# Two-stage attention and a rational feed-forward block: the denominator as |h| times a factor made by GpSimd, and a word's sign mask made by ScalarE

## The chip, the core and the metric

The kernel runs on one core of a Trainium2 chip. The core has a TensorE (PE in the profile; PEld is its loading of weights, which overlaps the matmuls), a VectorE (DVE), a ScalarE (ACT), a GpSimd (POOL) and a SyncE (SP), which here only issues DMAs. The metric is the device time of one execution in microseconds. Matmuls write to PSUM, which DVE and ACT read and POOL does not use; everything else is in SBUF.

## The reference, cut to what matters

```python
def sm_attn(qq, kk, vv):                       # float32, 8 batches x 8 heads, head size 64
    s = scale * np.matmul(qq, kk.transpose(0, 1, 3, 2))
    s = s - np.max(s, axis=-1, keepdims=True)
    a = np.exp(s)
    a = a / (np.sum(a, axis=-1, keepdims=True) + 1e-09)
    return np.matmul(a, vv)
p_packed = sm_attn(p, k, v)                    # 32 packed queries, 576 keys
x = sm_attn(q, p_packed, p_packed)             # 576 queries, 32 packed keys -> 4608 x 512 tokens
h = x @ w_in                                   # 512 -> 2048, w_in is float64
P = a[0] + a[1] * h + a[2] * h2 + a[3] * h3    # h2 = h*h, h3 = h*h*h
Q = 1.0 + np.abs(b[0]) * np.abs(h) + np.abs(b[1]) * h2
out = (P / (Q + 1e-06)) @ w_out                # 2048 -> 512, w_out is float64
```

The two weight matrices arrive as 64-bit floating-point words and have to be turned into 32-bit ones on the chip. The factor 8 on several inputs makes the numbers large; the kernel carries the polynomials scaled by S = 2**-40.

## The kernel before, in words

**Units.** The feed-forward part is cut into 128 units: 8 batches (`bb`), 2 halves of 288 tokens (`x`), 8 chunks of 256 hidden features (`c`). `hidden(bb, x, c)` does one unit in steps. For each half `f` of 128 features, PE sums `h` (128x288) in one of two PSUM banks; ACT reads `h` three times and writes `Y` (a3 h + a2), `U` (b0 |h|) and `sq` (the square, scaled by the root of b1); DVE makes `Y = Y h`, then `Y = (Y + a1) h`. After the second half POOL adds `U = U + sq` over 128x576; ACT takes Ln of U plus a constant and Exp of minus that, which gives an approximate reciprocal `V` in PSUM; DVE adds a0 and multiplies by V, refines V by one Newton step with `V = (U + c) V` and `Y = (2 - V) Y`. ACT rounds Y to `gh`, POOL subtracts to get `gl`, and `acc_block`, three units later (`LAG`), multiplies both with the weights of `w_out`. The first 12 units (`PLAIN`) instead use full float32 matmuls and need no gh and gl. `U` has two buffers, `sq` one, `Y` three, `V` one, `h` two.

**The scales.** `constants()` prepares the numbers. The scale a3 of `Y`, b0 of `U` and the root of b1 of `sq` are loaded into ScalarE registers (`reg_a3`, `reg_b0`, `reg_root`); the root takes a small chain of one-column operations on the tile `root`. The bias a2 and the operands a0, a1 are [128, 1] pointers into `abS`.

**The words.** `convert()` turns 16 blocks of 128x1024 words into float32, 8 of `w_in` and 8 of `w_out`. With `hi` and `lo` the two 32-bit halves of a word: ACT rescales `hi` as a float, ACT scales `lo` as an unsigned integer into the destination, DVE masks the sign bit of `hi` into `lo` (TENSOR_SCALAR in the profile), DVE shifts `hi` by three and ors the sign in (SCALAR_TENSOR_TENSOR), and DVE adds the two integers (CUSTOM_DVE_ANT_0; ISA in the order). The raw words lie in tiles called `m` and `w`, which serve other purposes later; the results go to `win`, `w` or `half`.

**The attention** of batch bb+1 is spread over 16 steps (`attention`, `filler`) among the units of batch bb; for batch 0 it stands ahead of everything and is the start of the program. `m_chunk` makes the matrices `m` that combine attention and `w_in`; `remainder` does the 64 rows of each batch that don't fill a tile of 128; `divide` splits the float32 blocks of `w_out` into a rounded part and a rest (ACT, then POOL on `w` and `half`).

**The order.** A class `Planner` collects all instructions, prices each (`cost`), builds the dependences (`edges`) and simulates the engines as lists: `schedule` forward with a rank for each instruction, then backward from the ends, which gives new ranks. `order` repeats this `ROUNDS` times and keeps the order with the earliest modelled end; `SLACK` is added to each hop between engines in the backward pass; `shares` names instructions of DVE that are modelled as locking GpSimd out of SBUF. Each engine then executes its instructions strictly in that order. Where the model sees PE without work in the first 150 us, `idle` puts matmuls with the tile `zero` there, which change no sum. All instructions go through one helper, so the profile shows one line, L288, for nearly all, and they are told apart by the names of their tiles.

Of the kernel before, what the change touches and what calls it, by code (L numbers as in the profile page):

```python
# [31 lines left out]
class Planner:  # L32
# [26 lines left out]
    FIRST = {"tensor": 700.0, "vector": 800.0, "scalar": 2000.0, "gpsimd": 1400.0, "sync": 700.0}  # L59
    ROUNDS = 8  # L60
    SWITCH = 95
    SLACK = 150
    IN_FLIGHT = 8
# [30 lines left out]
    def cost(self, engine, name, args, kwargs):  # L94
# [7 lines left out]
        if engine == "scalar":  # L102
            fixed += (aps[-1].space == PSUM) * -42 + ("accum_out" in kwargs) * 93 + ("bias" in kwargs) * 93
            per += 0.1 * any(x.ap[-1][0] == 2 for x in aps[:2])
        if engine == "gpsimd" and len(aps) < 3:
            fixed, per = 135, 0.9
        if engine == "vector" and len(aps) > 2 and any(self.columns(x) == 1 for x in aps[1:]):
# [82 lines left out]

    def schedule(self, before, after, rank, back=False):

# [13 lines left out]
        while left:  # L206
            for e in self.ENGINES:
# [26 lines left out]
                for j in after[i]:  # L234
                    need[j] -= 1
                    f = self.ops[j][0]
                    way = self.WAY.get((f, e) if back else (e, f), self.PASS)
                    way += self.SLACK * (back and way > 0)
                    at[j] = max(at[j], end[i] + way)
# [9 lines left out]
    def order(self):  # L249
# [7 lines left out]
        for i, x in enumerate(before):  # L257
            for j in x:
                after[j].append(i)
        rank = list(range(n))  # L260
        best = None
        for r in range(self.ROUNDS):
            start, end = self.schedule(before, after, rank)
            if best is None or max(end) < best[0]:
                best = self.best = max(end), start, end
            s, e = self.schedule(after, before, [-x for x in end], True)
            m = max(e)
            rank = [m - x for x in e]
            rank[: self.pinned] = range(-self.pinned, 0)
        self.end, self.start = best[0], best[1]  # L270
# [49 lines left out]
def attention_rational_ffn(  # L320
# [46 lines left out]
    make_identity(tc.nc, ident)  # L367
    ab, abS, one, root = (sb.tile([P, n], F32, name=x) for n, x in ((6, "ab"), (7, "abS"), (1, "one"), (5, "root")))
    zero = sb.tile([P, D], F32R, name="zero")
# [28 lines left out]
    def constants():  # L398
# [9 lines left out]
        nc.vector.tensor_scalar(m, m, 2.0**-126, None, ALU.max)  # L408
        nc.vector.tensor_scalar(e.bitcast(I32), m.bitcast(I32), 23, None, ALU.logical_shift_right)
        nc.vector.tensor_scalar(e.bitcast(I32), e.bitcast(I32), 127, None, ALU.add)  # L410
        nc.vector.tensor_scalar(p.bitcast(I32), e.bitcast(I32), 1, 23, ALU.logical_shift_right, ALU.logical_shift_left)
        nc.vector.reciprocal(i, p)
        nc.vector.tensor_scalar(m, m, i, i, ALU.mult, ALU.mult)
        nc.scalar.activation(r, m, AF.Ln)
        nc.scalar.activation(r, r, AF.Exp, scale=0.5)
        nc.vector.reciprocal(i, r)
        nc.vector.scalar_tensor_tensor(r, m, i, r, ALU.mult, ALU.add)
        nc.vector.tensor_scalar(abS[:, 6:7], r, p, 0.5 * S**0.5, ALU.mult, ALU.mult)
# [3 lines left out]
    a0, a1, a2, b0 = (abS[:, i : i + 1] for i in (0, 1, 2, 4))  # L422

    reg_a3, reg_b0, reg_b1, reg_root = (tc.nc.scalar.alloc_register(x) for x in ("a3", "b0", "b1", "root"))

# [65 lines left out]
    def convert():  # L491
# [384 lines left out]
    def hidden(bb, x, c):  # L876
# [5 lines left out]
        for f in range(2):  # L882
# [220 lines left out]
```

## Time and profile before

| | |
|---|---|
| median of 3 runs | 781.16 us (780.78 to 782.17) |
| profiled execution | 780.48 us, span in the trace 778.7 us |
| PE busy | 743.9 us, 96% of the span |
| DVE busy | 690.6 us, 89% |
| ACT busy | 654.8 us, 84% |
| POOL busy | 451.8 us, 58% |
| DMA | 56.04 MB, mean 72 GB/s |

The profiled execution is 1.8 us longer than its span (what lies before the first and behind the last instruction) and 0.7 us under the median. A busy share says how much of the span an engine's instructions cover; neighbouring instructions overlap a little on ACT and DVE, and the matmuls' ends are modelled, so 100% is full and 96% of PE is an average over a start with gaps and a body without.

### The profile page before, as it was taken

What the parts mean: (1) busy time and instruction counts of PE and PEld (TensorE: products, weight loads), DVE (VectorE), ACT (ScalarE), POOL (GpSimd) and SP (SyncE); (2) the same over time, 40 slices, a digit from 0 to 9 for tenths busy, and PEclk for the clock granted to TensorE, in tenths of its full rate; (3) what the DMA queues carried; (4) which work ended last, traced back from release to release, by engine and by line L of the source; (5) the groups of instructions that cost most, each with busy time, mean ns of one, the idle gap of its engine ahead of it and who ended that gap; (6) DMA issues with size and microseconds to landing.
All of it is one profiled execution on the core that took longest, in us unless ns stands there. A gap on an engine that the chain in (4) does not pass through costs nothing.

```text
span 778.7 us, 15003 instructions
## 1 busy us (share of the span) xinstructions
PE 743.9 (96%) x5350; PEld 569.8 (73%) x5350; DVE 690.6 (89%) x1295; ACT 654.8 (84%) x1464; POOL 451.8 (58%) x448
## 2 busy tenths in 40 slices
PE   2769999999999999999999999999999999999997
PEld 2435554678788787778788787778778787778886
DVE  4899999987998879998998889998999789998872
ACT  5889978998887988998897898998898798898881
POOL 0012357756695556765596556855586556856663
PEclk9979999999999999999999999999999999999999
DMA  9984260023601155022701128021801023000001
GB/s 299 369 272 145 103 122 28 1 86 53 105 1 55 45 60 98 1 86 38 120 1 55 45 38 120 1 64 41 112 27 55 34 46 40 14 12 17 28 0 42
DMA packets 152028, 56.04 MB, mean 72 GB/s; under 512 B 122256, under 2 KB 141200, under 8 KB 151952
## 3 DMA queue, kind: packets, MB, share of 16 engines
q1 hardware_dynamic: 151952, 55.07, 30.3%
q8 instruction: 42, 0.69, 0.4%
q14 instruction: 34, 0.28, 0.1%
HBM read 45.62 MB, written 9.44 MB: 71 GB/s over the span
## 4 chain that ended last, share of the span: by engine, by line
PE 71%; DVE 12%; ACT 11%; DMA 2%; issue 2%; POOL 1%; SPq 0%; DVEq 0%; ACTq 0%; POOLq 0%
PE acc L288 37%; PE h L288 22%; PE at L288 12%; DVE Y L288 4%; DVE w L288 2%; ACT V L288 2%; ACT Y L288 2%; DVE small L288 2%; DVE kx L288 2%; DMA nat<-in_k_dram 2%; ACT U L288 2%; ACT sq L288 1%; ACT half L288 1%; ACT w L288 1%; DVE V L288 1%
## 5 line engine op out<-in xcount | busy, mean ns | idle before, releaser
L288 POOL TENSOR_TENSOR U<-U,sq 128x576 f32<-128x576 f32 x128 | 184.9, 1444 | 102.1 <-ACT U L288 47.5
L288 PE MATMUL acc<-w,gh 128*128 128x512 f32 x736 | 236.9, 406 | 0.3
L288 PE MATMUL h<-AH,m 128*128 128x288 f32 x1024 | 200.6, 318 | 4.7 <-DVE Y L288 4.0
L288 PEld LDWEIGHTS h<-AH,m 128*128 128x128 f32 x1024 | 160.0, 189 | 45.8 <-DVE Y L288 24.5
L288 POOL TENSOR_TENSOR gl<-Y,gh 128x512 fp32r<-128x512 f32 x116 | 150.4, 1296 | 46.1 <-ACT gh L288 15.2
L288 PEld LDWEIGHTS acc<-w,gh 128*128 128x128 f32 x736 | 133.5, 188 | 44.0 <-issue 9.0
L288 ACT ACTIVATE Y<-h,abS 128x288 f32<-128x288 f32 x256 | 128.5, 518 | 25.0 <-PE h L288 20.1
L288 PE MATMUL acc<-w,gl 128*128 128x512 f32 x384 | 148.1, 412 | 0.2 <-DVE w L288 0.2
L288 ACT ACTIVATE sq<-h 128x288 f32<-128x288 f32 x256 | 108.9, 428 | 34.9 <-PE h L288 26.7
L288 DVE TENSOR_TENSOR Y<-Y,h 128x288 f32<-128x288 f32 x256 | 109.0, 444 | 26.7 <-ACT sq L288 11.6
L288 DVE SCALAR_TENSOR_TENSOR Y<-Y,abS,V 128x576 f32<-128x576 f32 x128 | 102.9, 804 | 27.5 <-ACT V L288 26.7
L288 DVE SCALAR_TENSOR_TENSOR Y<-Y,abS,h 128x288 f32<-128x288 f32 x256 | 124.7, 505 | 2.2
L288 ACT ACTIVATE U<-h 128x288 f32<-128x288 f32 x256 | 102.5, 432 | 11.2 <-DVE V L288 7.4
L288 ACT ACTIVATE V<-U,one 128x576 f32<-128x576 f32 x128 | 99.4, 777 | 10.8 <-DVE Y L288 7.9
L288 PE MATMUL h<-AL,m 128*128 128x288 f32 x448 | 96.0, 295 | 0.0
L288 DVE SCALAR_TENSOR_TENSOR V<-U,V 128x576 f32<-128x576 f32 x128 | 95.8, 749 | 0.0
L288 DVE SCALAR_TENSOR_TENSOR Y<-V,Y 128x576 f32<-128x576 f32 x116 | 86.3, 744 | 1.4
L288 PEld LDWEIGHTS acc<-w,gl 128*128 128x128 f32 x384 | 71.3, 188 | 20.1 <-issue 6.4
L288 ACT ACTIVATE V<-V 128x576 f32<-128x576 f32 x128 | 85.5, 668 | 0.4
L288 PE MATMUL acc<-half,gh 128*128 128x512 f32 x240 | 78.7, 409 | 0.0
L288 ACT CAST gh<-Y 128x512 fp32r<-128x512 f32 x116 | 73.7, 635 | 2.0 <-DVE Y L288 1.3
L288 PEld LDWEIGHTS h<-AL,m 128*128 128x128 f32 x448 | 71.8, 188 | 0.6 <-issue 0.5
(135 smaller groups left out, 955.5 us busy)
## 6 DMA issues: line engine op xcount, KB each, us to landing
w<-in_moe_w_out_dram SPq DMA_DIRECT2D x16, 512.0 KB, 4.4
out_dram<-half SPq DMA_DIRECT2D x15, 512.0 KB, 3.1
nat<-in_k_dram SPq DMA_DIRECT2D x48, 144.0 KB, 3.8
nat<-in_q_dram SPq DMA_DIRECT2D x48, 144.0 KB, 4.3
nat<-in_v_dram SPq DMA_DIRECT2D x24, 256.0 KB, 3.3
m<-in_moe_w_in_dram SPq DMA_DIRECT2D x8, 512.0 KB, 5.7
w<-in_moe_w_in_dram SPq DMA_DIRECT2D x8, 512.0 KB, 9.6
nat<-in_k_dram SPq DMA_DIRECT2D x4, 512.0 KB, 8.5
```

The lines of the kernel that those rows point to most:

```text
L288: getattr(getattr(self.nc, engine), name)(*args, **kwargs)
```

## The change

The denominator |b0| |h| + |b1| h*h becomes |h| (b0 + b1 |h|). ACT no longer writes `sq`; `U` is now |h| without a scale; POOL makes the factor with one TENSOR_SCALAR (times b1, plus b0, both [128, 1] pointers) into the tile that was `sq`, and a multiplication takes the place of the addition. The root and the ScalarE registers go away, so the scale of `Y` is a pointer too.

In `convert`, the sign mask is made by ACT: a leaky rectification (Prelu) of `hi` as a float with scale 2**-40 and a slope of 2**90 for negative values, written into the integer `lo`; positive words come out as 0 and negative ones as the lowest integer, which is the sign bit. It has to read `hi` ahead of the rescaling in place and write `lo` behind the scaling of `lo`, so the three ACT instructions stand in a new sequence.

The planner is changed with it: `SLACK` becomes five values that are each tried for 6 rounds in place of one value for 8; the one-input price of GpSimd (135 + 0.9 per column) now holds for its TENSOR_SCALAR with pointers; and `shares` now names every DVE instruction with two wide SBUF operands.

```diff
-    ROUNDS = 8
+    ROUNDS = 6
-    SLACK = 150
+    SLACK = 60, 100, 150, 220, 300
-        if engine == "gpsimd" and len(aps) < 3:
-            fixed, per = 135, 0.9
+        if engine == "gpsimd" and sum(self.columns(x) > 1 for x in aps) < 3:
+            fixed, per = (135, 0.9)
...
-        return name in ("tensor_scalar", "tensor_copy") or (name == "tensor_add" and aps[0].dtype == I32)
+        wide = sum(self.columns(x) > 8 for x in aps[1:])
+        return wide > 1 or name in ("tensor_scalar", "tensor_copy")
...
-        for r in range(self.ROUNDS):
-            start, end = self.schedule(before, after, rank)
+        for slack in self.SLACK:
+            start, end = first
+            for r in range(self.ROUNDS):
+                s, e = self.schedule(after, before, [-x for x in end], slack)
...
-        m, e, p, r, i = (root[:, n : n + 1] for n in range(5))
-        nc.vector.scalar_tensor_tensor(m, ab[:, 5:6], -1.0, ab[:, 5:6], ALU.mult, ALU.max)
...
-        for i, reg in enumerate((reg_a3, reg_b0, reg_b1, reg_root)):
-            nc.scalar.reg_load(reg, abS[0:1, 3 + i : 4 + i].bitcast(I32))
...
+        nc.scalar.activation(di, lo.bitcast(U32), AF.Copy, scale=2.0**-29)
+
+        nc.scalar.activation(lo, hi.bitcast(F32), AF.Prelu, scale=2.0**-40, alpha=2.0**90)
         nc.scalar.activation(hi.bitcast(F32), hi.bitcast(F32), AF.Copy, scale=REBIAS)
-
-        nc.scalar.activation(di, lo.bitcast(U32), AF.Copy, scale=2.0**-29)
-        nc.vector.tensor_scalar(lo, hi, -0x80000000, None, ALU.bitwise_and)
         nc.vector.scalar_tensor_tensor(hi, hi, 3, lo, ALU.logical_shift_left, ALU.bitwise_or)
         nc.vector.tensor_add(dst.bitcast(I32), hi, di)
...
-            nc.scalar.activation(y, h, AF.Identity, scale=reg_a3, bias=a2)
-            nc.scalar.activation(u, h, AF.Abs, scale=reg_b0)
-            nc.scalar.activation(U2[:, f, :], h, AF.Square, scale=reg_root)
+            nc.scalar.activation(y, h, AF.Identity, scale=a3, bias=a2)
+            nc.scalar.activation(u, h, AF.Abs)
...
             if f == 1:
-                nc.gpsimd.tensor_add(U, U, U2)
+                nc.gpsimd.tensor_scalar(U2, U, b1, b0, ALU.mult, ALU.add)
+                nc.gpsimd.tensor_mul(U, U, U2)
```

The new order at three places; the numbers behind a name count tiles and differ by one between the two programs. First ACT around unit 70 in the body of the program, before:

```order
L288 ACTIVATE sq_70_914<-h_139_915 128x288
L288 ACTIVATE U_70_911<-h_139_915 128x288
L288 ACTIVATE Y_70_913<-h_139_915,abS 128x288
L288 ACTIVATE V_69_902<-U_69_901,one 128x2x288
L288 CAST gh_62_918<-Y_68_888 128x512
L288 ACTIVATE V_69_902<-V_69_902 128x2x288
L288 ACTIVATE U_70_911<-h_140_917 128x288
L288 ACTIVATE kx_6_865,small<-at_131_899,small 128x288
L288 ACTIVATE kx_6_865,small<-at_132_900,small 128x288
L288 ACTIVATE sq_70_914<-h_140_917 128x288
L288 ACTIVATE Y_70_913<-h_140_917,abS 128x288
```

The same place after, from the first read of the same `h` on:

```order
L293 ACTIVATE U_70_910<-h_139_914 128x288
L293 ACTIVATE V_69_901<-U_69_900,one 128x2x288
L293 ACTIVATE Y_70_912<-h_139_914,abS 128x288
L293 ACTIVATE V_69_901<-V_69_901 128x2x288
L293 ACTIVATE kx_6_864,small<-at_131_898,small 128x288
L293 ACTIVATE U_70_910<-h_140_916 128x288
L293 ACTIVATE Y_70_912<-h_140_916,abS 128x288
L293 ACTIVATE kx_6_864,small<-at_132_899,small 128x288
```

From each `h` two reads are left of three; `U` stands first, and the rounding to `gh` has moved behind both reads of `Y`.

POOL in the same unit, before:

```order
L288 TENSOR_TENSOR U_70_911<-U_70_911,sq_70_914 128x576
L288 COPY G<-Y_69_903 128x2x32
L288 TENSOR_TENSOR gl_63_929<-Y_69_903,gh_63_928 128x512
L288 TENSOR_TENSOR U_71_920<-U_71_920,sq_71_923 128x576
L288 COPY G<-Y_70_913 128x2x32
```

and after:

```order
L293 TENSOR_SCALAR sq_70_913<-U_70_910,abS 128x576
L293 TENSOR_TENSOR U_70_910<-U_70_910,sq_70_913 128x576
L293 TENSOR_TENSOR gl_62_918<-Y_68_887,gh_62_917 128x512
L293 COPY G<-Y_69_902 128x2x32
L293 TENSOR_SCALAR sq_71_922<-U_71_919,abS 128x576
```

One instruction more per unit, and `gl` of an older unit now stands behind the U of unit 70.

DVE at the first unit of the program, where the conversion of words is under way, before:

```order
L288 TENSOR_SCALAR w_5_119<-w_5_119 128x1024
L288 TENSOR_TENSOR Y_1_127<-Y_1_127,h_1_129 128x288
L288 TENSOR_TENSOR Y_1_127<-Y_1_127,h_2_132 128x288
L288 SCALAR_TENSOR_TENSOR Y_1_127<-Y_1_127,abS,h_1_129 128x288
L288 SCALAR_TENSOR_TENSOR w_5_119<-w_5_119 128x1024
L288 SCALAR_TENSOR_TENSOR Y_1_127<-Y_1_127,abS,h_2_132 128x288
L288 TENSOR_SCALAR w_7_121<-w_7_121 128x1024
L288 ISA w_10_161<-w_5_119,w_10_161 128x2048
```

and after:

```order
L293 SCALAR_TENSOR_TENSOR w_4_117<-w_4_117 128x1024
L293 TENSOR_TENSOR Y_1_126<-Y_1_126,h_1_128 128x288
L293 ISA win<-w_4_117,win 128x2048
L293 SCALAR_TENSOR_TENSOR Y_1_126<-Y_1_126,abS,h_1_128 128x288
L293 TENSOR_TENSOR Y_1_126<-Y_1_126,h_2_131 128x288
L293 SCALAR_TENSOR_TENSOR Y_1_126<-Y_1_126,abS,h_2_131 128x288
L293 SCALAR_TENSOR_TENSOR w_5_118<-w_5_118 128x1024
L293 ISA w_10_160<-w_5_118,w_10_160 128x2048
```

Each block has lost its mask (TENSOR_SCALAR), and one block more than before is still being converted when the first unit begins: `w_4` was done by then, now it stands among the first unit's instructions.

More of the change, by code (lines that the diff above doesn't have):

```diff
@@ L104, in cost @@
             per += 0.1 * any(x.ap[-1][0] == 2 for x in aps[:2])
-        if engine == "gpsimd" and len(aps) < 3:
-            fixed, per = 135, 0.9
+        if engine == "gpsimd" and sum(self.columns(x) > 1 for x in aps) < 3:
+            fixed, per = (135, 0.9)
+            if name == "tensor_scalar":
+                fixed, per = (135, 0.9)
         if engine == "vector" and len(aps) > 2 and any(self.columns(x) == 1 for x in aps[1:]):
@@ L189, in edges, with schedule @@
         return edges
-    def schedule(self, before, after, rank, back=False):
+    def schedule(self, before, after, rank, back=0):
         n = len(rank)
@@ L237, in schedule @@
                     way = self.WAY.get((f, e) if back else (e, f), self.PASS)
-                    way += self.SLACK * (back and way > 0)
+                    way += back * (way > 0)
                     at[j] = max(at[j], end[i] + way)
@@ L259, in order @@
                 after[j].append(i)
-        rank = list(range(n))
+        first = self.schedule(before, after, list(range(n)))
         best = None
-        for r in range(self.ROUNDS):
-            start, end = self.schedule(before, after, rank)
[L264 to L269, printed above, removed]
+        for slack in self.SLACK:
+            start, end = first
+            for r in range(self.ROUNDS):
+                s, e = self.schedule(after, before, [-x for x in end], slack)
+                m = max(e)
+                rank = [m - x for x in e]
+                rank[: self.pinned] = range(-self.pinned, 0)
+                start, end = self.schedule(before, after, rank)
+                if best is None or max(end) < best[0]:
+                    best = self.best = max(end), start, end
         self.end, self.start = best[0], best[1]
@@ L367, in attention_rational_ffn @@
     make_identity(tc.nc, ident)
-    ab, abS, one, root = (sb.tile([P, n], F32, name=x) for n, x in ((6, "ab"), (7, "abS"), (1, "one"), (5, "root")))
+    ab, abS, one = (sb.tile([P, n], F32, name=x) for n, x in ((6, "ab"), (6, "abS"), (1, "one")))
     zero = sb.tile([P, D], F32R, name="zero")
@@ L404, in constants @@
         nc.vector.memset(one, (1.0 + 1e-6) * S)
-        m, e, p, r, i = (root[:, n : n + 1] for n in range(5))
-        nc.vector.scalar_tensor_tensor(m, ab[:, 5:6], -1.0, ab[:, 5:6], ALU.mult, ALU.max)
[L408 to L418, printed above, removed]
-        for i, reg in enumerate((reg_a3, reg_b0, reg_b1, reg_root)):
-            nc.scalar.reg_load(reg, abS[0:1, 3 + i : 4 + i].bitcast(I32))
-    a0, a1, a2, b0 = (abS[:, i : i + 1] for i in (0, 1, 2, 4))
-    reg_a3, reg_b0, reg_b1, reg_root = (tc.nc.scalar.alloc_register(x) for x in ("a3", "b0", "b1", "root"))
+    a0, a1, a2, a3, b0, b1 = (abS[:, i : i + 1] for i in range(6))
     words = [(kind, 2 * c, 2) for kind in ("in", "out") for c in range(NCH)]
```

## The prediction

> **What bounds the kernel now.** I first cut the span into stretches (busy time of each engine in each stretch), because the page's averages mix a start, a stage that converts words and a long body.
>
> ```profile
> core 0: us, PE busy (x) PEld busy (x) DVE busy (x) ACT busy (x) POOL busy (x), PEclk, DMA share, GB/s
> 0.00:36.00 36.00, 17.25 (x233) 12.51 (x234) 22.74 (x48) 24.32 (x42) 1.70 (x7) 0.95 1.01 333
> 36.00:57.00 21.00, 13.59 (x83) 7.91 (x84) 20.13 (x36) 17.70 (x34) 2.77 (x3) 0.76 0.87 276
> 57.00:143.00 86.00, 85.17 (x542) 46.02 (x541) 85.50 (x160) 77.14 (x164) 45.08 (x35) 1.00 0.35 96
> 160.00:757.00 597.00, 593.34 (x4332) 477.39 (x4332) 538.23 (x1014) 514.25 (x1182) 384.19 (x389) 1.00 0.25 48
> ```
>
> From 36 to 143 us DVE is the bound: 20.13 of 21 and 85.50 of 86 us. PE looks full from 57 us on too, but its ends are modelled, so the waits decide which of the two leads:
>
> ```profile
> ACT Y L288 <- PE h L288: 7.1, 6, 1.9
> PEld acc L288 <- issue: 13.0, 46, 0.8
> PEld h L288 <- DVE Y L288: 2.9, 6, 0.9
> ```
>
> Those are from 57 to 143 us: ACT waits 7.1 us for `h`, PE's loads have holes, and DVE itself waits for nothing over 0.4 us. DVE sets the pace, the others follow. In the body, 160 to 757 us, PE leads with 593 of 597 us and DVE has 59 us free. What PE still waits for there, in the groups of weight loads and in the waits of DVE:
>
> ```profile
> L288 PEld LDWEIGHTS h<-AH,m 128*128 128x128 f32 x879 | 133.4, 188 | 30.9 <-DVE Y L288 18.8 <-DVE kx L288 1.7 <-issue 1.4
> ...
> DVE Y L288 <- ACT V L288: 25.1, 41, 2.4
> DVE Y L288 <- ACT sq L288: 11.0, 15, 1.0
> DVE Y L288 <- ACT U L288: 9.1, 18, 1.0
> DVE Y L288 <- ACT Y L288: 4.1, 5, 0.9
> ```
>
> The loads of `h` wait 18.8 us for DVE to have read an `h` bank, and DVE waits 11.0 + 9.1 + 4.1 us for ACT at that same place: the round is PE, ACT, DVE, PE, with two banks. So ACT's reads of `h` reach the end of the program through at most 18.8 us, though ACT is not the fullest engine.
>
> **The change part by part.** The instructions concerned, by group:
>
> ```profile
> L288 POOL TENSOR_TENSOR U<-U,sq 128x576 f32<-128x576 f32 x128 | 184.9, 1444 | 102.1 <-ACT U L288 47.5 <-ACT sq L288 34.4 <-DVE Y L288 8.8
> L288 ACT ACTIVATE sq<-h 128x288 f32<-128x288 f32 x256 | 108.9, 428 | 34.9 <-PE h L288 26.7 <-POOL U L288 6.9 <-POOL gl L288 0.8
> L288 DVE TENSOR_SCALAR w<-w 128x1024 int32<-128x1024 int32 x12 | 9.0, 753 | 0.0
> L288 DVE TENSOR_SCALAR m<-m 128x1024 int32<-128x1024 int32 x4 | 2.8, 697 | 8.0 <-ACT win L288 8.0
> L288 POOL COPY G<-Y 128x64 f32<-128x64 f32 x116 | 27.7, 239 | 74.1 <-DVE Y L288 65.6 <-ACT half L288 5.3 <-PE acc L288 2.4
> L288 POOL COPY pn<-pn x8: 284/295/992, 13.6 to 517.1; 128x128 f32<-128x128 f32 x8
> ```
>
> ACT's and DVE's neighbours overlap, so on a full engine an instruction costs its distance to the next start, which the timeline gives:
>
> ```profile
> 48.24 0.45 ACT L288 ACTIVATE sq<-h 128x288 f32<-128x288 f32 x1
> 48.53 0.46 ACT L288 ACTIVATE U<-h 128x288 f32<-128x288 f32 x1
> ...
> 70.22 1.35 ACT L288 ACTIVATE w<-w 128x1024 f32<-128x1024 f32 x1
> 71.25 0.62 ACT L288 ACTIVATE sq<-h 128x288 f32<-128x288 f32 x1
> ...
> 53.48 0.50 ACT L288 ACTIVATE Y<-h,abS 128x288 f32<-128x288 f32 x1 [0.78 <-PE h L288]
> 53.88 0.40 ACT L288 ACTIVATE U<-h 128x288 f32<-128x288 f32 x1
> ...
> 86.52 0.69 DVE L288 TENSOR_SCALAR w<-w 128x1024 int32<-128x1024 int32 x1
> 87.13 0.15 DVE L288 TENSOR_TENSOR small<-small 128x4 f32<-128x4 f32 x1
> ...
> 75.26 2.01 POOL L288 TENSOR_TENSOR U<-U,sq 128x576 f32<-128x576 f32 x1 [4.74 <-ACT sq L288]
> ...
> 76.28 1.56 DVE L288 TENSOR_SCALAR w<-w 128x1024 int32<-128x1024 int32 x1
> 77.76 0.50 DVE L288 SCALAR_TENSOR_TENSOR Y<-Y,abS,h 128x288 f32<-128x288 f32 x1
> ```
>
> So a `sq` is worth 0.29 us of ACT, a 1024-wide ACTIVATE 1.03, and a mask 0.61 us of DVE; `Y` with one [128, 1] pointer takes 0.11 more than `sq` with none.
>
> *The scale of Y as a second pointer.* No row has two. Bounds: nothing, and the 0.11 us of the first pointer twice. I take 0.11 us, 256 times.
>
> *Prelu.* Not in the trace. Bounds: the 1.03 us of the same width, and 1.4 us, the longest that such rows stand on ACT (1.35 above). I take 1.03: nothing in the rows tells one function from another.
>
> *POOL's TENSOR_SCALAR over 576 columns with two pointers.* Not in the trace. The nearest one-input rows are the copies, 239 ns for 64 columns and 295 (the median) for 128: 0.875 ns a column, so 0.69 us for 576 as the low end; the high end is the two-input 1.44 us. I take 0.69, since it reads one tile. The multiplication costs what the addition did.
>
> Stage one, 36 to 143 us. I count 11 of the 16 masks there (the other five come while DVE waits for ACT or DMA, as the 8.0 us of the `m` group show): 10 of 0.61 and the one that took 1.48 to the next start, 7.6 us less on a full DVE. ACT gains 11 Prelu x 1.03 = 11.3 us and 30 pointers x 0.11 = 3.3 us and loses 30 `sq` x 0.29 = 8.7 us (15 units), so 5.9 us more. It has 3.3 + 8.9 = 12.2 us free in the two stretches; 6.3 us stay. The stage can shrink by at most 6.3 us before ACT is full, by 7.6 before DVE is as full as now. With both tight I take 5 us; bounds 0 (below) and 7.6.
>
> Ahead of it, 0 to 36 us: five Prelu more on ACT. By the order, eight 1024-wide ACTIVATEs come ahead of the first copy of the transposed keys where there were six; the extra two fall into ACT's waits for DMA:
>
> ```profile
> ACT m L288 <- DMA m<-in_moe_w_in_dram: 6.3, 3, 3.9
> ```
>
> Counting to the first unit's `Y`, three more are placed; the third lies among copies that PE and DVE wait for. I add 1 us (0 to 3.1). The root's chain, twelve one-column instructions of DVE, two of ACT and the register loads, goes; it lay beside this work, and I count it as nothing, since each is 0.2 us or less and the DVE waits here anyway. The planner's idle matmuls (`zero`) go from 19 rows to 38 in the order. I cost them at nothing because they stand where PE has no data; if PE had data, the 38 instructions of 4 us that the trace shows now would become 8.
>
> The body holds 110 units (`sq` on ACT, then on POOL, from 160 to 757 us):
>
> ```profile
> 160.00:757.00 597.00, 91.48 (x219) 156.38 (x110) 1.00 0.25 48
> ```
>
> 219 `sq` go and 0.11 us per `Y` comes: ACT has about 0.36 us less per unit. What that is worth is bounded by 18.8 us, PE's waits for DVE's `Y`, and by nothing. Where `sq` stood ahead of `Y` in the order (as in unit 70) DVE's two steps start 0.29 us earlier, and DVE's 11.0 us for `sq` vanish, while its 9.1 us for `U` may stay. I take 8 us, somewhat under half. PE's own arithmetic is unchanged, so nothing beyond the waits can be had there. If ACT's `U` is done earlier, the next to be late is POOL: its chain is one TENSOR_SCALAR longer. POOL has 384 of 597 us, and 110 x 0.69 make it 460, 77%. Who waits for POOL's U today, in the waits of the whole span:
>
> ```profile
> ACT sq L288 <- POOL U L288: 6.9, 12, 0.9
> ACT V L288 <- POOL U L288: 1.8, 2, 1.2
> ```
>
> The first was for the one `sq` buffer, which only POOL will use. The second says that Ln nearly always finds U done. In the order `U` is read off `h` first and `sq` no longer follows, 0.3 to 0.4 us earlier, so Ln sees some 0.3 us more delay; behind it in ACT's queue stand the next unit's reads of `h`. I count nothing for it, and cost it as a rival.
>
> Sum, against the profiled execution of 780.48 us (span 778.7 and 1.8 around it): -5 + 1 - 8 = -12, 768.5 us. The median of the runs lies 0.7 above that execution, so 769.2 us.
>
> **A rule against the change.** The pair at 75.26 and 76.28 us shows POOL's U at 2.01 us and DVE's mask, begun inside it, at 1.56 us where others take 0.69. The Trainium skill, page "SBUF — State Buffer", section "Who interferes with whom", says that DVE in a two-port mode, or with two SBUF inputs, shares a port pair with GpSimd that is locked for a whole instruction, and the second one "fully blocks". By that rule POOL's new instruction, which reads SBUF, opens more collisions with the two DVE steps of a conversion that stay; the trace agrees with it in this pair, where the mask lost 0.87 us. By the rule carried through all conversions the sum would be that of rival (b); by the rows' own durations it is the -12 above.
>
> **The rivals.**
>
> (a) *PE's floor.* In the body the waits of PE have another cause: DVE's 25.1 us for `ACT V` stay, and the `h` bank is released no earlier. For it: DVE's `Y` is not behind `sq` in all units. Then -5 + 1 = -4, 777.2 us.
>
> (b) *The port.* In stage one 22 DVE steps of conversions (two each for 11 blocks) remain, on a full DVE. If each loses 0.35 us to POOL, about what separates two such rows today (below), 7.7 us are gone and with them the 7.6 us of the masks: 0 + 1 - 8 = -7, 774.2 us. Against it: POOL is busy for only 45 of 86 us there.
>
> ```profile
> 103.75 1.57 DVE L288 SCALAR_TENSOR_TENSOR w<-w 128x1024 int32<-128x1024 int32 x1
> 58.33 1.22 DVE L288 SCALAR_TENSOR_TENSOR w<-w 128x1024 int32<-128x1024 int32 x1
> ```
>
> (c) *POOL becomes the bound: slower.* If the TENSOR_SCALAR costs 1.44 us, POOL gets 384 + 110 x 1.44 = 542 of 597 us, 91%, and more in the attention steps of each batch, where it has these besides:
>
> ```profile
> L288 POOL TENSOR_TENSOR kx<-kx,small 128x576 f32<-128x576 f32 x28 | 32.5, 1163 | 18.8 <-DVE small L288 18.8
> L288 POOL TENSOR_TENSOR AL<-kx,AH 128x576 fp32r<-128x576 f32 x14 | 20.1, 1436 | 1.8 <-ACT AH L288 1.8
> L288 POOL TENSOR_TENSOR gl<-Y,gh 128x512 fp32r<-128x512 f32 x116 | 150.4, 1296 | 46.1 <-ACT gh L288 15.2 <-PE acc L288 11.2 <-issue 10.4
> ```
>
> Eight units then need 8 x (1.44 + 1.44 + 1.30 + 0.24) + 4 x 1.16 + 2 x 1.44 = 42.9 us of POOL in 8 x 597/110 = 43.4 us. In a strict order an engine that is 99% full makes others wait; 2 us for each of seven batches, and no gain in the body: 14 - 5 + 1 = +10, 791.2 us. It decides from about 1.2 us per TENSOR_SCALAR, where these stretches are 95% full.
>
> (d) *The change does not do what it says.* Prelu at 1.4 us and the second pointer at 0.22 fill ACT: 15.4 + 6.6 - 8.7 = 13.3 us more against 12.2 free. ACT then keeps stage one as long as it is, the start loses 1, and the pointers eat most of the `sq` in the body: no change, 781 us.
>
> (e) *The whole of it.* All 18.8 us of PE's waits go, and 5 in stage one: 780.48 + 0.7 - 18.8 - 5 + 1 = 758.4 us.
>
> **How the numbers follow.** The forecast has 0.50, (a) 0.18, (b) 0.08, (c) 0.12, (d) 0.06, (e) 0.06. The likeliest is 769.2 us, with 765 to 773 as its own range (3 us less or more of the body's 8, 1 of stage one's 5). The range for the whole is 758 to 782: it holds all cases but (c) and the edges of (e) and (d). Faster by over 0.2% (1.6 us, about what a measurement of this kernel can tell from no change): the forecast, (a), (b) and (e), 0.82, less 0.02 for (a) falling short, 0.80. Slower: (c) and a third of (d), 0.14. The rest, 0.06, is within 0.2%.
>
> **What would show it.** DVE from 36 us to where it stops being full should end near 138 us in place of 143, with 16 fewer TENSOR_SCALARs of 128x1024; ACT should be over 95% there. POOL's TENSOR_SCALAR should read 0.6 to 0.8 us. PEld's wait of `h` for `DVE Y` should fall from 18.8 to about 10 us, and no engine should wait over some 5 us for `POOL U`. I am wrong if that last wait grows to tens of us (c), if DVE's conversion steps lengthen from 1.22 to 1.6 us throughout (b), or if stage one ends no earlier with ACT full (d).

## The result, and the profile after

The changed kernel takes 799.57 us (median of 4 runs, 798.46 to 799.77), the kernel before 780.97 us on the same chip: a ratio of 1.0233, with a 95% interval of 1.0221 to 1.0246. It is slower by 18.6 us where 12 us less were forecast. The profiled execution is the one of 798.46 us (span 796.7). All medians and ratios leave out two executions of some 4000 us, one of two_factors and one of the kernel before beside two_or. The stretches of the changed kernel, with the columns of the first fence of the prediction:

```profile
0.00:36.00 36.00, 15.22 (x232) 10.63 (x232) 19.05 (x36) 26.43 (x41) 1.46 (x7) 1.00 1.02 321
36.00:57.00 21.00, 13.84 (x98) 7.54 (x99) 16.56 (x28) 19.70 (x36) 5.67 (x5) 0.80 0.93 313
57.00:143.00 86.00, 85.41 (x548) 49.38 (x547) 81.43 (x151) 81.44 (x145) 47.96 (x41) 0.99 0.35 92
160.00:757.00 597.00, 586.25 (x4256) 461.46 (x4249) 522.06 (x992) 455.07 (x939) 456.70 (x482) 1.00 0.26 48
```

In stage one DVE is no longer full (16.56 of 21 and 81.43 of 86 us, before 20.13 and 85.50), as the removal of the masks should make it. In the body every engine but POOL is less busy than before: DVE 522, ACT 455, PE 586 us. POOL went from 384 to 457. No engine is full, so something waits. The chain of work that ended last, before and then after, shares of the span by engine:

```profile
PE 71%; DVE 12%; ACT 11%; DMA 2%; issue 2%; POOL 1%; SPq 0%; DVEq 0%; ACTq 0%; POOLq 0%
```

```profile
PE 31%; ACT 24%; DVE 18%; POOL 16%; issue 5%; DMA 4%; SPq 1%; POOLq 0%; ACTq 0%; DVEq 0%
```

PE carried 71% of that chain and now carries 31%; POOL went from 1 to 16%. The waits and groups that answer to those of the prediction:

```profile
POOL sq L293 <- ACT U L293: 108.8, 81, 5.1
ACT V L293 <- DVE Y L293: 40.3, 32, 3.4
ACT V L293 <- POOL U L293: 34.0, 34, 2.5
```

```profile
L293 POOL TENSOR_SCALAR sq<-U,abS x128: 811/823/1436, 48.5 to 776.2; 128x576 f32<-128x576 f32 x128
L293 PEld LDWEIGHTS h<-AH,m 128*128 128x128 f32 x848 | 126.7, 188 | 32.4 <-DVE Y L293 21.9 <-issue 1.2 <-DVE small L293 0.8
L293 ACT ACTIVATE w<-w 128x1024 int32<-128x1024 f32 x12 | 14.4, 1200 | 0.0
L293 ACT ACTIVATE w<-w 128x1024 f32<-128x1024 f32 x12 | 14.4, 1202 | 0.0
```

ACT's Ln waits 34.0 us in 34 places for POOL's U, where it waited 1.8 us in 2. POOL itself waits 108.8 us for ACT's U. Two engines that wait for each other, both with idle time, suggest a round, and the timelines of ACT and POOL show one, without another wait in between (a unit late in the body):

```profile
653.98 0.75 ACT L293 ACTIVATE V<-U,one 128x576 f32<-128x576 f32 x1 [0.61 <-POOL U L293]
654.75 0.64 ACT L293 ACTIVATE V<-V 128x576 f32<-128x576 f32 x1
655.30 0.41 ACT L293 ACTIVATE U<-h 128x288 f32<-128x288 f32 x1
655.59 0.60 ACT L293 ACTIVATE Y<-h,abS 128x288 f32<-128x288 f32 x1
656.07 0.42 ACT L293 ACTIVATE U<-h 128x288 f32<-128x288 f32 x1
...
659.03 0.75 ACT L293 ACTIVATE V<-U,one 128x576 f32<-128x576 f32 x1 [1.10 <-POOL U L293]
```

```profile
656.66 0.82 POOL L293 TENSOR_SCALAR sq<-U,abS 128x576 f32<-128x576 f32 x1 [1.29 <-ACT U L293]
657.57 1.43 POOL L293 TENSOR_TENSOR U<-U,sq 128x576 f32<-128x576 f32 x1
```

Ln at 653.98, Exp, U and Y of the next unit's first half, U of its second half until 656.49; POOL's factor from 656.66 and product until 659.00; the next Ln at 659.03. That is 5.05 us a unit, set by ACT and POOL in turn. It is not the pace of every unit: of the 109 distances from one Ln to the next in the body, 14 lie between 5.03 and 5.10 us and 20 are shorter.

To see where the 18.6 us are, I read the start of the first `Y` of three units from ACT's timeline (unit 18 is where the body begins; one profiled execution each):

| run | unit 0 | unit 18 | unit 127 | body, 18 to 127 | median |
|---|---|---|---|---|---|
| before | 47.6 | 161.6 | 757.3 | 595.7 | 780.97 |
| after | 46.7 | 164.0 | 775.9 | 611.8 | 799.57 |
| no_pointer | 46.2 | 162.1 | 766.7 | 604.6 | 790.43 |
| no_factor | 47.8 | 164.3 | 764.8 | 600.5 | 787.2 |
| no_pointer_no_factor | 46.9 | 162.1 | 757.7 | 595.6 | 780.37 |
| new_order | 51.4 | 163.7 | 762.9 | 599.1 | 783.05 |
| den_only | 50.7 | 168.5 | 783.5 | 615.0 | 804.62 |
| mask_relu | 53.2 | 162.0 | 760.0 | 597.9 | 778.58 |
| before_halves_Y4 | 49.5 | 163.8 | 759.6 | 595.8 | 783.21 |
| two_or | 46.4 | 161.6 | 755.7 | 594.1 | 779.15 |

The changed kernel loses 2.4 us up to unit 18 and 16.1 us in the body. The other rows are the experiments.

### The profile page after: what moved, and what is told of

Its sections match the earlier page's. It is cut to its first block, busy times and chain, and to the rows that moved or that the text cites. A ratio compares the mean times of both kernels' runs of the same rounds, so it can differ in the third digit from the quotient of the medians.

```text
span 796.7 us, 15046 instructions
## 1 busy us (share of the span) xinstructions
PE 752.4 (94%) x5388; PEld 568.5 (71%) x5388; DVE 677.0 (85%) x1269; ACT 615.5 (77%) x1222; POOL 552.4 (69%) x576
## 4 chain that ended last, share of the span: by engine, by line
PE 31%; ACT 24%; DVE 18%; POOL 16%; issue 5%; DMA 4%; SPq 1%; POOLq 0%; ACTq 0%; DVEq 0%
PE acc L293 15%; DVE Y L293 11%; PE h L293 10%; ACT V L293 9%; PE at L293 6%; POOL U L293 6%; ACT Y L293 4%; POOL sq L293 4%; ACT U L293 4%; DVE V L293 3%; POOL gl L293 3%; ACT w L293 2%; DMA m<-in_moe_w_in_dram 2%; ACT gh L293 2%; DVE kx L293 1%
## 5 line engine op out<-in xcount | busy, mean ns | idle before, releaser
L293 POOL TENSOR_SCALAR sq<-U,abS 128x576 f32<-128x576 f32 x128 | 106.1, 829 | 130.0 <-ACT U L293 108.8
L293 PEld LDWEIGHTS h<-AH,m 128*128 128x128 f32 x1024 | 157.9, 189 | 47.6 <-DVE Y L293 28.0
L293 POOL TENSOR_TENSOR U<-U,sq 128x576 f32<-128x576 f32 x128 | 183.8, 1436 | 9.5
L293 ACT ACTIVATE Y<-h,abS 128x288 f32<-128x288 f32 x256 | 148.8, 595 | 22.4 <-PE h L293 14.6
L293 ACT ACTIVATE V<-U,one 128x576 f32<-128x576 f32 x128 | 96.1, 751 | 81.1 <-DVE Y L293 40.3
L293 DVE TENSOR_TENSOR Y<-Y,h 128x288 f32<-128x288 f32 x256 | 112.6, 447 | 19.5 <-ACT U L293 11.2
L293 ACT ACTIVATE U<-h 128x288 f32<-128x288 f32 x256 | 100.9, 409 | 15.5 <-DVE V L293 9.1
L293 ACT CAST gh<-Y 128x512 fp32r<-128x512 f32 x116 | 72.0, 621 | 27.6 <-DVE Y L293 14.9
L293 ACT ACTIVATE V<-V 128x576 f32<-128x576 f32 x128 | 82.7, 646 | 0.8
```

Of the source, the lines that this page charges most:

```text
L293: getattr(getattr(self.nc, engine), name)(*args, **kwargs)
```

## The experiments

**Is it POOL's step or the order?** Two runs keep the order of all engines' instructions word for word and change only what POOL issues; two exchange the planner.

`no_factor`, at the place where an instruction is issued:

```diff
+                if engine == "gpsimd" and str(args[0].tensor.tag)[:2] == "sq":
+                    continue
+                # ... and the multiplication takes U, U in place of U, sq
```

> The changed kernel with every engine's order kept, but GpSimd's TENSOR_SCALAR is not issued and the multiplication takes U twice (the factor b0 + b1 |h| is left out, U becomes |h| squared). Chain theory (a unit's path U, POOL, Ln, Exp, Y got 0.83 us longer and the body pays for it): Ln's wait for POOL U falls from 34 us to under 5, the time falls by 12 to 18 us of the 18.6 lost, 782 to 788 us. Order theory (the sequence of the instructions is what costs): the time stays at 795 to 800 us though POOL has 106 us less to do.

`two_factors` issues that TENSOR_SCALAR twice.

> The changed kernel with every engine's order kept, and the TENSOR_SCALAR issued twice, so that POOL's chain per unit is another 0.83 us longer (POOL about 552 + 106 = 658 of the span). Chain theory: the loss of the 0.83 us is repeated or more, 815 to 830 us, and ACT's wait for POOL U grows from 34 to 60 us and more. Order theory: under 5 us more, 800 to 805 us, since POOL is not full.

`old_order` and `new_order` exchange `Planner` between the two kernels (the old one with the new one-input price of GpSimd).

> The changed arithmetic, ordered by the planner's old search (one slack of 150, 8 rounds) and old list of DVE instructions that lock GpSimd; GpSimd's one-input price as in the changed kernel. Order theory: 768 to 783 us, the loss is gone. Chain theory: 795 to 802 us, the loss stays whoever orders it.

> The arithmetic of before (ACT's square, POOL's addition, DVE's mask, registers), ordered by the changed planner (five slacks of 6 rounds, the longer list of locking DVE instructions). Order theory: 793 to 800 us, the loss comes with the search alone. Chain theory: 776 to 784 us, no loss without the longer POOL step.

Measured: no_factor 787.2 us (ratio 1.0067, 1.0046 to 1.0089), two_factors 881.42 (1.1276, 1.1249 to 1.1303), old_order 799.07 (1.0213, 1.0189 to 1.0238), new_order 783.05 (1.0029, 1.0014 to 1.0045). The order theory falls: the old search keeps the loss, and the new search without the new arithmetic costs 2 us. POOL's step matters, and not in proportion: taking one away gives 12.4 us, adding one costs 82, far over the 815 to 830 us that the chain theory expected. In two_factors the distance from Ln to Ln grows by the added step:

```profile
ACT V L294 <- POOL U L294: 133.6, 80, 3.5
...
729.01 0.75 ACT L294 ACTIVATE V<-U,one 128x576 f32<-128x576 f32 x1 [2.48 <-POOL U L294]
...
735.00 0.75 ACT L294 ACTIVATE V<-U,one 128x576 f32<-128x576 f32 x1 [2.21 <-POOL U L294]
```

5.99 us in place of 5.05, about the 0.83 of the step and the 0.09 of the gap behind it. The body of before needs 595.7 / 109 = 5.47 us a unit on average, so a round of 5.05 can hold back only units with little other work, and one of 5.99 nearly all. The distances from Ln to Ln bear that out in part. Over the last 16 units, which have no attention of a next batch beside them, they sum to 75.5 us before, 85.4 after and 99.3 in two_factors; from unit 18 to 111 to 515.1, 525.7 and 587.3. So 9.9 of the 20.5 us that the changed kernel loses by these starts lie in those 16 units. One reservation on no_factor: its multiplication of U by itself ran faster than that of two tiles (the row below, 1153 ns against 1436), so it took about 1.1 us off each unit's POOL work, not 0.83, and the factor alone is probably worth less than 12.4 us.

```profile
L297 POOL TENSOR_TENSOR U<-U 128x576 f32<-128x576 f32 x128 | 147.6, 1153 | 158.8 <-ACT U L297 156.2 <-DVE Y L297 1.6 <-POOL AL L297 0.8
```

**Which half of the change?** `den_only` puts DVE's mask back; `mask_relu` is the kernel before with the changed planner and the mask by ACT.

```diff
 den_only:
+        nc.scalar.activation(hi.bitcast(F32), hi.bitcast(F32), AF.Copy, scale=REBIAS)
         nc.scalar.activation(di, lo.bitcast(U32), AF.Copy, scale=2.0**-29)
-        nc.scalar.activation(lo, hi.bitcast(F32), AF.Prelu, scale=2.0**-40, alpha=2.0**90)
-        nc.scalar.activation(hi.bitcast(F32), hi.bitcast(F32), AF.Copy, scale=REBIAS)
+        nc.vector.tensor_scalar(lo, hi, -0x80000000, None, ALU.bitwise_and)
 mask_relu (on before): the reverse, with
+        nc.scalar.activation(lo, hi.bitcast(F32), AF.Relu, scale=2.0**-40)
```

> The changed denominator, scales and planner, with DVE's mask of before. If the denominator carries the whole loss: 797 to 803 us, and Prelu alone is worth the small rest either way. If the mask has a part in it (it should have gained 5 us by the forecast, or lost some 6 us that the run without the factor leaves unexplained): 804 to 808 us, or 792 to 795 us.

> The denominator, scales and registers of before, the changed planner, and the word's mask by ACT, with a plain rectification (Relu) in the place of Prelu, which leaves out the sign of negative words. The forecast's step for the mask (5 us less in stage one, 1 us more ahead of it): 4 us under the run that has the new order alone, 777 to 780 us. Rival: ACT's three steps of a conversion stand in one queue and DVE waits for the third, so nothing is won, 782 to 786 us.

den_only took 804.62 us (1.0303, 1.0274 to 1.0332), mask_relu 778.58 (0.9963, 0.9947 to 0.9979). So the mask by ACT gains 5.0 us (804.62 to 799.57) with the one denominator and 4.5 us (783.05 to 778.58) with the other, and the denominator carries more than the whole loss. All four are planned anew, so these differences hold what the order does too.

**Can the round be cut?** `u_first` adds one rule to the planner; `halves` shortens POOL's path.

```diff
 u_first:
+        for u, i in self.ln.items():                 # index of a unit's Ln
+            if u + 1 in self.read:                   # index of a unit's last read of h on ACT
+                edges[i].add(self.read[u + 1])
 halves:
-            if f == 1:
-                nc.gpsimd.tensor_scalar(U2, U, b1, b0, ALU.mult, ALU.add)
-                nc.gpsimd.tensor_mul(U, U, U2)
+            nc.gpsimd.tensor_scalar(U2[:, f, :], u, b1, b0, ALU.mult, ALU.add)
+            nc.gpsimd.tensor_mul(u, u, U2[:, f, :])
```

> The changed kernel, with one more rule for the planner: a unit's Ln stands on ACT behind the next unit's second read of h into U (in the changed kernel that read stands behind Ln in 98 of 109 units of the body). Loop theory (Ln, Exp, the next U, POOL's TENSOR_SCALAR and multiplication, Ln form a closed round of 5.05 us, which is longer than PE's work of a unit): the round is cut, ACT's wait for POOL U falls from 34 to under 8 us and the time to 780 to 788 us. Theory of the strict queues (wherever the reads stand, POOL's 0.83 us more per unit come out as another wait, as with the old search, where ACT waited 55 us for POOL gl): 794 to 800 us, with ACT or PE waiting for POOL gl instead.

> The changed kernel, but GpSimd does factor and multiplication for each half of 288 columns as soon as ACT has written it, four instructions of about 0.52 and 0.77 us in place of two of 0.83 and 1.44. From the second read of h to Ln there are then about 1.3 us of POOL in place of 2.27, though POOL has about 0.3 us more per unit (some 595 us busy of the span). Chain theory: 778 to 787 us. Theory of POOL's load (it is the work and not the length of the path that counts): 802 to 812 us.

u_first took 799.0 us (1.0231, 1.02 to 1.0262), halves 810.5 (1.0377, 1.0354 to 1.0401). The loop theory fails: ACT's wait for POOL U fell from 34.0 to 2.3 and 8.3 us, and nothing was gained. halves, which gave POOL 66 us more work, lies where the theory of POOL's load had it. Another wait has taken the place of the first, as the theory of the strict queues said (6.7 us in the changed kernel); u_first first, then halves:

```profile
ACT Y L297 <- POOL gl L297: 39.3, 37, 2.1
```

```profile
ACT Y L293 <- POOL gl L293: 72.5, 62, 2.6
```

(In old_order the same wait has 55.5 us.) `gl` is the last reader of a unit's `Y`, and `Y` has three buffers: ACT may not write `Y` before POOL has come to the `gl` of three units ago. So I asked whether it is POOL's work or the number of buffers. `extra_after_gl` adds work of nearly the same size off the path from U to Ln; `halves_Y4` is halves with a factor tile of 288 columns, which leaves room for a fourth `Y`.

```diff
 extra_after_gl, behind each issued gl:
+                    self.nc.gpsimd.tensor_scalar(self.again, self.again, 1.0, 0.0, ALU.mult, ALU.add)   # the last sq
 halves_Y4:
-    ... (("U", 2), ("sq", 1), ("Y", 3)))
+    ... (("U", 2), ("sq", 1), ("Y", 4)))
+    U2_ring = Ring(sb, "sq", 1, [P, HALF])
```

> The changed kernel with every engine's order kept, and one more TENSOR_SCALAR of 128x576 on GpSimd (times 1, plus 0, in place) behind each of its 116 subtractions gl: about the work that the doubled factor added (0.74 to 0.83 us a unit), but outside the path from a unit's U to its Ln. Theory of the path (a round of ACT and POOL in which POOL itself idles 1.28 us a unit): the extra falls into that idle time, 799 to 806 us. Theory of the load (POOL's work as such costs): 860 to 885 us, as with the factor doubled (883).

> The run with POOL's work in halves (810.5 us), and a fourth buffer for Y, made room for by a factor tile of 288 columns. There ACT waited 72 us for POOL gl, which reads Y before Y's buffer comes free. If it is the three buffers of Y that keep ACT in step with POOL: that wait falls under 20 us and the time to 785 to 797 us. If POOL's work is what counts, the wait moves elsewhere: 806 to 813 us.

```profile
L297 POOL TENSOR_SCALAR sq<-sq 128x576 f32<-128x576 f32 x116 | 78.8, 680 | 0.0
```

extra_after_gl took 821.88 us (1.0523, 1.0505 to 1.054): 22 us for 78.8 us of added work, where the same kind of work on the path cost 82 us for 106. Both theories missed: the place counts, but off the path is not free. POOL takes its instructions in order, so the added one also holds up the next unit's factor: Ln's wait for POOL U grew from 34.0 to 53.4 us. halves_Y4 took 790.2 us (1.0122, 1.0105 to 1.0138), 20 us under halves with the same POOL work (622.8 us busy, 79% of its span; 618.6 in halves), and `Y` now waits for PE instead of `gl`:

```profile
L293 ACT ACTIVATE Y<-h,abS 128x288 f32<-128x288 f32 x256 | 152.3, 599 | 56.9 <-PE h L293 49.7 <-POOL sq L293 1.2 <-POOL gl L293 1.1
```

That POOL is too full is thereby refuted. What costs, as far as these runs show, is the time from a unit's first instruction to the release of its buffers, over a fixed number of buffers; that no single hold explains the whole loss is what u_first showed.

`before_factor` adds the TENSOR_SCALAR to the kernel before, in its order, on `sq` ahead of the addition. `mask_ptr` is before with the changed planner, Prelu for the mask, and pointers for the three scales.

> The kernel before with every engine's order kept, and a TENSOR_SCALAR of 128x576 with two pointers on sq ahead of POOL's addition (which changes the denominator's value): the longer POOL step alone, with ACT's square, registers and DVE's mask as they were. If the POOL step carries the loss: 797 to 815 us. If the square's removal or the pointers on ACT have a part in it: under 792 us.

> The mask by Prelu with the old denominator (ACT's square, POOL's addition) and the changed planner; the three scales are [128, 1] pointers in place of registers, some 0.08 us more for each of 768 reads of h on ACT. If the mask's gain stands (the run with Relu had 778.6) and ACT has room for the pointers: 777 to 783 us. If ACT, then some 92% busy in the body, becomes the limit: 788 to 800 us.

before_factor took 822.92 us (1.0533, 1.0516 to 1.0551), above both expectations and above the changed kernel. Its order was planned without the step, and with `sq` on ACT a second wait comes up, for the one `sq` buffer; which of the two makes it slower than the changed kernel was not tested:

```profile
ACT sq L290 <- POOL U L290: 42.7, 45, 1.9
```

mask_ptr took 811.46 us (1.0389, 1.0372 to 1.0406), above both expectations and 33 us above mask_relu. It differs from that run in the pointers, in Prelu for Relu (1237 against 1253 ns on the blocks in `w`, so not dearer) and in the order planned with them:

```profile
L293 ACT ACTIVATE Y<-h,abS 128x288 f32<-128x288 f32 x256 | 157.5, 628 | 15.2 <-PE h L293 11.6 <-POOL gl L293 3.1
L293 ACT ACTIVATE sq<-h,abS 128x288 f32<-128x288 f32 x256 | 136.9, 538 | 20.6 <-PE h L293 14.1 <-POOL U L293 4.8 <-POOL G L293 1.2
L293 ACT ACTIVATE U<-h,abS 128x288 f32<-128x288 f32 x256 | 129.3, 535 | 5.0 <-DVE V L293 3.0 <-PE h L293 1.6
```

Each pointer adds about 0.11 us to a read of `h` (`sq` 428 ns before, 538 here). So Y's second pointer had to be a suspect in the changed kernel too.

**Pointer and factor at one order.** `no_pointer` keeps the order of the changed kernel and issues `Y` with the constant `S` for its scale; `no_pointer_no_factor` does that and no_factor together; `den_reg` is den_only with a3 in ACT's register.

> The changed kernel with every engine's order kept, and the scale of Y a constant in the instruction in place of a [128, 1] pointer (a3 is left out). Y's reads of h should fall from 595 to some 515 ns. If the pointer has a part in the loss (two Y reads lie between Exp and the second read of U in the round of 5.05 us, 0.16 to 0.22 us a unit): 785 to 794 us. If ACT's idle time, 23%, covers it: 797 to 801 us.

> The same with the TENSOR_SCALAR left out as well, every order kept (b0, b1 and a3 are left out). The run without the factor alone stood at 787.2, 6.6 us above before. If the pointer is the rest: 776 to 782 us. If the rest lies in the order or in the start: 785 to 788 us.

> The changed denominator with DVE's mask (804.6 us), and the scale of Y in a register of ACT as before; planned anew. If the pointer has a part: 792 to 799 us, and what stays above the run with the new order alone (783) is POOL's step. If not: 803 to 806 us.

```profile
L295 ACT ACTIVATE Y<-h,abS 128x288 f32<-128x288 f32 x256 | 125.3, 502 | 25.4 <-PE h L295 16.3 <-POOL gl L295 7.1 <-POOL U L295 1.3
```

```profile
L293 ACT ACTIVATE Y<-h,abS 128x288 f32<-128x288 f32 x256 | 148.8, 595 | 22.4 <-PE h L293 14.6 <-POOL gl L293 6.7 <-POOL G L293 0.2
```

The first row is no_pointer, the second the changed kernel: 502 against 595 ns. no_pointer took 790.43 us (1.012, 1.0093 to 1.0147), no_pointer_no_factor 780.37 (0.9989, 0.9975 to 1.0003), den_reg 798.55 (1.0214, 1.0188 to 1.0241). At one order the pointer costs 9.1 us, POOL's factor with the slower multiplication 12.4, both together 19.2, and the body goes from 611.8 by 604.6 or 600.5 to 595.6, where before stood (595.7). Planned anew, the register is worth 6.1 us (804.62 to 798.55).

**A version that beats both.** Three more came from these findings. `before_halves_Y4` gives the kernel before a fourth `Y` by adding in halves. `mask_zero` and `two_or` keep the old denominator and take DVE's mask away in other ways.

```diff
 mask_zero:
+        nc.scalar.activation(lo.bitcast(F32), hi.bitcast(F32), AF.Copy, scale=2.0**-100)
 two_or (before's planner):
-        nc.scalar.activation(di, lo.bitcast(U32), AF.Copy, scale=2.0**-29)
-        nc.vector.tensor_scalar(lo, hi, -0x80000000, None, ALU.bitwise_and)
-        nc.vector.scalar_tensor_tensor(hi, hi, 3, lo, ALU.logical_shift_left, ALU.bitwise_or)
-        nc.vector.tensor_add(dst.bitcast(I32), hi, di)
+        nc.scalar.activation(di, lo.bitcast(U32), AF.Copy, scale=2.0**-29 * (1 - 2.0**-12), bias=-0.4999)
+        nc.vector.scalar_tensor_tensor(di, hi, 3, di, ALU.logical_shift_left, ALU.bitwise_or)
+        nc.vector.scalar_tensor_tensor(di, hi, -0x80000000, di, ALU.bitwise_and, ALU.bitwise_or)
```

> The kernel before, with POOL's addition done in halves of 288 columns, so that sq needs half its tile and Y gets a fourth buffer; planner of before. If Y's buffers hold PE back in the kernel before too (PE waits 18.8 us for DVE's Y in the body): 766 to 776 us, faster than both kernels. If PE's work is the floor there or the halves cost POOL as much as the buffer gives: 779 to 786 us.

> The denominator, scales and registers of before, the changed planner, and the sign mask by ACT in a third way: the rescaled high half times 2**-100 underflows to a zero that keeps its sign, and a negative zero is the word 0x80000000. It costs the 1.03 us of a wide ACTIVATE like Prelu and Relu. By the run with Relu (0.9963 of before): 777 to 780 us, faster than both kernels. If the mask's place behind the rescaling makes the conversion's chain longer by one ACTIVATE and DVE waits for it: 781 to 785 us.

> The kernel before, its planner too, with a conversion of two DVE steps in place of three and no more ACT work: ACT scales lo to a whole number from 0 to 7 (rounded down, where before it rounded and could carry), DVE shifts hi by three and ors that number in, and ors the sign bit of hi into the sum; the mask and the integer addition go. What Relu and the two other masks by ACT showed is that 16 masks less on DVE are worth 4 to 5 us in the start and stage one. If that holds without ACT's 16 added steps: 773 to 778 us, faster than both kernels. If the start is bound by other things: 779 to 782 us.

before_halves_Y4 took 783.21 us (1.0018, 1.0005 to 1.0031): nothing gained, though PE's wait for DVE's Y fell as the forecast had it for the change (the body of that run):

```profile
L288 PEld LDWEIGHTS h<-AH,m 128*128 128x128 f32 x876 | 134.9, 188 | 30.8 <-DVE Y L288 10.7 <-DVE small L288 2.6 <-ACT gh L288 1.7
```

mask_zero took 779.64 us (0.9967, 0.9955 to 0.9979), but its output is off by the same amount as that of mask_relu (33.38, relative), which writes no sign. So the zero did not keep its sign, and mask_zero is no replacement. two_or took 779.15 us (0.9966, 0.9953 to 0.9978): faster than the kernel before by 0.3% (2.7 us) and than the changed one by 20 us. Its low words are rounded down where before they were rounded to the nearest. It gains less than the 5 us of the mask. By its unit starts it is 1.8 us ahead at unit 11 (119.8 against 121.6), no longer at unit 18, and 1.6 us shorter in the body (594.1 against 595.7), which is as fine as two single profiles can tell; where its gain comes from is not shown.

## Why the prediction was wrong, step by step

**DVE bounds stage one: the mask's sum came out, its place only in one pair.** Two pairs of runs give 5.0 and 4.5 us against the 5 - 1 of the sum. By the table, mask_relu against new_order begins unit 0 1.8 us later and is 3.5 us shorter from there to unit 18, as the step had it. The changed kernel against den_only begins unit 0 4.0 us earlier and is 0.5 us shorter from there to unit 18: the right size there is in part luck. Prelu takes what its neighbours take (1200 and 1202 ns), so rival (d) had no base there. Yet stage one of the changed kernel ended no earlier: unit 18 starts 2.4 us late. At this order Y's pointer is 1.9 us of that (164.0 to 162.1); den_only begins unit 18 at 168.5, so the denominator took back there about what the mask gave (new_order begins it at 163.7). ACT had 81.44 of 86 us, 94.7% and not over 95.

**The body's gain of 8 us: failed.** The step read 18.8 us of PE's waits for DVE's `Y` as time that could be had. But those are waits of the weight loads, which overlap the matmuls. The matmuls themselves waited this long in the kernel before, from 160 to 778 us:

```profile
PE h L288 <- DVE Y L288: 2.8, 4, 1.3
```

And the step's own row has PE busy for 593.34 of 597 us, which leaves 3.7 us and not 8 (with ends that are modelled). In no_pointer_no_factor, which has neither `sq` nor pointer nor factor, and in before_halves_Y4 that wait is 11.0 and 10.7 us in the body, and the body takes 595.6 and 595.8 us, as before. Shorter waits of the weight loads did not make PE end earlier. That there is nothing to gain in the body is what rival (a), PE's floor, said; that the body would lose, it did not. In the changed kernel the wait is 21.9 us. The row of no_pointer_no_factor:

```profile
L299 PEld LDWEIGHTS h<-AH,m 128*128 128x128 f32 x876 | 132.6, 188 | 22.6 <-DVE Y L299 11.0 <-issue 0.9 <-DVE small L299 0.8
```

**POOL's longer chain, counted as nothing: the step that cost most.** The sum took "Ln nearly always finds U done" for slack that would remain. It does not say how much slack there is, and with `U` 0.83 us later Ln waits 34 us. At one order this is 12.4 us (with the faster multiplication of that run in it). The price was of less weight: 0.69 us forecast, 0.823 measured. What the longer step met is not Ln alone: where Ln was moved out of the way (u_first), `Y` waited for POOL's `gl` and the time stayed.

**Y's second pointer: priced about right, placed wrongly.** 0.11 us was taken; it measures 0.09 (595 - 502 ns; 503 with the register in den_reg). The step set it against the `sq` that go and kept a gain of 0.36 us per unit of ACT's time. But two such reads stand in the round from Ln to Ln, where ACT's gain by the missing `sq` did not help: 9.1 us at one order.

**Rival (c)** came nearest with 791.2 us, by a mechanism that is not the one found: it made POOL full from about 1.2 us per TENSOR_SCALAR. The step takes 0.823 us, POOL has 457 of 597 us in the body, and halves_Y4 is 20 us faster than halves at the same load. The wait that (c) named as its sign, tens of us for `POOL U`, is there all the same.

**Rival (b) and the rule on the port.** The steps of conversion on DVE, before and after:

```profile
L288 DVE SCALAR_TENSOR_TENSOR w<-w 128x1024 int32<-128x1024 int32 x12 | 15.4, 1286 | 0.0
```

```profile
L293 DVE SCALAR_TENSOR_TENSOR w<-w 128x1024 int32<-128x1024 int32 x12 | 15.8, 1317 | 2.6 <-ACT w L293 2.6
```

0.03 us more each, against the 0.35 of the rival. POOL was hardly busier there (47.96 against 45.08 us from 57 to 143), so the test is a weak one. The Trainium skill, page "SBUF — State Buffer", section "Who interferes with whom", would let the second engine wait for a whole instruction. These rows do not show more of that than before.

**What stays open.** The squares' removal by itself at the order of before was not run; the nearest, 780.37 us without `sq` and 778.58 with it, have different orders and show no gain. no_pointer_no_factor has the mask by ACT too and is no faster than before; where its 4 to 5 us went was not taken apart. The new order alone costs 2 us. Nor is the body of no_pointer_no_factor that of before in its parts: by the Ln starts it is 2.2 us shorter from unit 18 to 111 and 5.8 us longer in the last 16 units. What the changed denominator costs in stage one beyond the pointer is not taken apart.

## What to carry to other kernels

An engine that is 60% full is no free place for work if the work lengthens the path on which a unit holds its buffers: price such a step by what the next instruction in the waiting queue loses, and count the round (here Ln, Exp, the next reads, POOL, Ln) against the time per unit of the leading engine. Cutting that one round by the order is not enough, as u_first showed; look at which buffer is released last. Waits of a leading engine's loads are no stock of time either: look at how long its matmuls wait, and test by a run that shortens the waits. And keep every part of a change apart in the sum, since here one half gained 4 to 5 us and the other lost over 20.

## What the runs showed of the hardware

GpSimd's TENSOR_SCALAR of 128x576 takes 823 ns with two pointers (median; 829 in place, before_factor) and 680 with two constants (in place, extra_after_gl), and a product of one tile with itself 1153 ns (no_factor) against 1436 for two tiles. A [128, 1] scale on ACT adds 0.09 to 0.11 us to a 128x288 read of PSUM over a constant (595 against 502 ns for `Y`) or a register (538 against 428 for `sq`). In mask_zero, an ACTIVATE of negative numbers that underflow (times 2**-100 behind a rescaling) gave zeros without their sign, as its output, off by as much as that of mask_relu, tells.
